# The first keys in two parts, and the sums, the spread and the first output block in other places: a change to a decode attention kernel

## The chip, the cores and the metric

The kernel runs on one core of a Trainium2 chip. The metric is the device time of one execution in microseconds (us). A profile is one execution taken by the hardware profiler; its span is some 2 us shorter than the time of the same run. "The change" is the edit under study, "the kernel before" is what it was made to.

## The reference, cut to what matters

One token attends over the last 4096 of 32768 cached positions in 32 heads; an MLP branch (not touched here) gates the result.

```python
W = min(4096, max(256, Sk // 4))
k = k_cache[:, :, Sk - W:, :]          # 32 heads x 4096 x 128, bf16: 33.6 MB
v = v_cache[:, :, Sk - W:, :]          # the same again
scores = einsum("bhqd,bhkd->bhqk", q, k) * Dh ** -0.5
p = softmax(scores)
o = einsum("bhqk,bhkd->bhqd", p, v)
s = o.reshape(B, Sq, Hq * Dh) @ wo     # wo is 4096 x 512
return x + s * g                       # g: the gate, from the MLP branch
```

## The kernel before

The 32 heads go in 8 groups of 4. A stage `s` does the scores of group `s`, the softmax of group `s-1` and the products with V of group `s-2`. Each group's keys (4.19 MB, 128 columns of rows) are split between two engines. VectorE does columns 0 to `nd` (64 or 80) in four quarters, each a product and a reduce (`k_vector`). TensorE transposes the rest in blocks of 8 columns (`k_turn`), ScalarE copies them out of PSUM, TensorE multiplies (`k_scores`).

```python
K_BUFS = 3; V_BUFS = 2                               # cut: other constants
ps_misc = tile_pool(name="ps_misc", bufs=1, space=PSUM)
ps_tr   = tile_pool(name="ps_tr",   bufs=3, space=PSUM)   # the transposes, tag "pt"

def sm_max(g):                                        # cut: VectorE, S <- own, m1 <- max of S
def sm_turn(g):
    mt_ps = ps_misc.tile([1, P], FP32, tag="misc", name="mt_ps")
    nc.tensor.transpose(mt_ps[:], s["m1"][:], ident_f[:])
    mx = sm_pool.tile([1, G], FP32, tag="mx", name="mx")
    nc.vector.tensor_reduce(out=mx[:], in_=mt_ps[:]...)   # cut; then md <- mx
def sm_exp(g):                                        # cut: mb_ps (misc) <- md on TensorE,
                                                      # 4 exponentials on ScalarE
def sm_den(g):
    s["den"] = ps_misc.tile([P, G], FP32, tag="misc", name="den_ps")
    nc.tensor.matmul(s["den"][:], lhsT=ones_f[:], rhs=s["sum"][:], start=True, stop=True)
def sm_rden(g):
    nc.vector.reciprocal(out=s["rden"][:], in_=s["den"][:])
```

`v_part` are the products with V. In groups 1 and 3 they are 32 wide matmuls into `ov`, whose result is put together one stage later. After group 3 the first 16 heads are done: `ox_spread(0)` (VectorE), `ox_pick(0)` (TensorE, then VectorE, over `ox_ps` in the misc pool) and `y_wide(0)` (16 wide matmuls into `yr_ps`) multiply them with the output weights in stage 6. In the code, `own` are the scores of TensorE's part, which ScalarE scales into SBUF; `mt_ps` is the transpose of the maxima, `mx` and `md` the maximum and its scaled negative for the exponentials; `spread` and `pick` bring the heads' outputs into the layout of the output weights. The order of this loop is the order of each engine's instructions:

```python
for s in range(NG + LAG):
    kn = load_kv(k_pool, A_k_cache, s) if s < NG else None
    # cut: loads of V, at the latest place the two V buffers allow
    if s < NG:
        k_vector(s, kn, 0); k_turn(s, kn, 0); k_turn(s, kn, 1); k_scores(s, 0)
        if s > 0:
            sm_turn(s - 1); k_turn(s, kn, 2); k_scores(s, 1); sm_exp(s - 1)
        # cut: v_add, v_out of groups 1 and 3
        if s == 6: ox_spread(0)
        k_vector(s, kn, 1)
        # cut: the remaining k_turn, k_scores
        sm_own(s)
        if s == 6: ox_pick(0)
        k_vector(s, kn, 2)
        if s > 0:
            sm_den(s - 1); sm_rden(s - 1)
        k_vector(s, kn, 3)
        if h >= 0: v_part(h, v)                       # h = s - 2
        sm_max(s)
        if s == 6: y_wide(0)
        # cut: v_out
    # cut: the two last stages
```

## Time and profile before

| | before |
|---|---|
| time, median of the 4 runs beside the change | 201.68 us (201.14 to 204.34) |
| span of the profile | 199.9 us |
| loads | 78.84 MB, 93.1% of the 16 DMA engines' time |
| VectorE busy | 73% |
| TensorE busy (matmul) | 67% |
| last V asked for | 178.05 us |

The highest of the four, 204.34, is 1.6% above the lowest and counts as slow; ratios leave such runs out, medians and ranges here do not.

The busy shares alone mislead: VectorE is the busiest compute engine, but the loads are busy nearly always. Which of them sets the end is read from the hole in the loads and from what the last loads wait for; the prediction shows these lines.

### The profile page before, as it was taken

How to read it: one execution, taken by the hardware profiler on the slowest of the kernel's cores; microseconds unless marked ns; L12 is line 12 of the kernel's file. 1: busy time of each engine (PE TensorE's matmuls, PEld its weight loads, DVE VectorE, ACT ScalarE, POOL GpSimd, SP SyncE). 2: the span in 40 equal slices, each digit the busy share in tenths (PEclk: the TensorE clock that was granted, in tenths of full speed). 3: DMA queues.
4: the chain of work that ended last, by engine and by line, in shares of the span. 5: the costliest groups of instructions: out<-in, count | busy, mean ns of one | idle time of the engine just before them, and what ended most of it. 6: DMA issues, size and time to landing. Idle time of an engine off the chain costs nothing.

```text
span 199.9 us, 4705 instructions
## 1 busy us (share of the span) xinstructions
PE 134.0 (67%) x2098; PEld 103.6 (52%) x2098; DVE 145.8 (73%) x160; ACT 85.3 (43%) x193; POOL 6.0 (3%) x13
## 2 busy tenths in 40 slices
PE   0459754953575268736997782789776876778582
PEld 0353544842465268635446782733576445766471
DVE  1640105999966999999999999999659999691201
ACT  2003004883687273528119752730792059723000
POOL 2110007000000000000000000000000000000000
PEclk9999855597555555555698755558965596555555
DMA  6999999999999999999999999999999999839850
GB/s 211 407 471 420 420 456 449 434 426 416 426 420 423 453 448 426 430 423 433 420 423 446 439 393 459 439 426 420 430 446 433 430 408 443 368 94 393 319 216 0
DMA packets 4891, 79.13 MB, mean 396 GB/s; under 512 B 648, under 2 KB 1512, under 8 KB 2024
## 3 DMA queue, kind: packets, MB, share of 16 engines
q1 hardware_dynamic: 4720, 78.84, 93.1%
q8 instruction: 16, 0.26, 0.5%
q10 hardware_dynamic: 152, 0.00, 0.0%
q14 instruction: 3, 0.02, 0.0%
HBM read 78.84 MB, written 0.00 MB: 394 GB/s over the span
## 4 chain that ended last, share of the span: by engine, by line
DVE 49%; PE 20%; DMA 16%; ACT 11%; issue 3%; ACTq 0%; DVEq 0%
DVE S L305 29%; DVE prod L303 15%; DMA kv<-in_A_k_cache_dram 14%; ACT kt L314 5%; PE ov L405 5%; ACT pT L357 4%; PE oT L413 4%; PE pt L312 4%; PE yr_ps L476 3%; PE sT L319 2%; DMA x_bf<-in_A_x_dram 2%; PE y_ps L152 1%; PE den_ps L363 1%; DVE S L333 1%; PE mb_ps L350 1%
## 5 line engine op out<-in xcount | busy, mean ns | idle before, releaser
L305 DVE TENSOR_REDUCE S<-prod 128x20 f32<-128x2560 bf16 (+1 forms) x32 | 83.8, 2619 | 1.1
L314 ACT COPY kt<-pt 128x1024 bf16<-128x1024 bf16 x54 | 53.3, 1013 | 18.5 <-PE pt L312 18.2
L312 PE MATMUL pt<-ident_bf,kv 128*128 128x128 bf16 x432 | 48.3, 286 | 3.5 <-DMA kv<-in_A_k_cache_dram 2.4
L303 DVE TENSOR_TENSOR prod<-kv,q_bc 128x2560 bf16<-128x2560 bf16 (+1 forms) x32 | 44.3, 1384 | 5.4 <-DMA kv<-in_A_k_cache_dram 5.1
L312 PEld LDWEIGHTS <-kv 128*128 128x128 bf16 x432 | 38.3, 130 | 5.7 <-issue 2.7
L319 PE MATMUL sT<-qT_bf,kt 128*128 128x4 bf16 x432 | 20.4, 169 | 18.6 <-ACT kt L314 18.3
L319 PEld LDWEIGHTS <-kt 128*128 128x128 bf16 x432 | 17.7, 107 | 24.6 <-ACT kt L314 24.1
L413 PEld LDWEIGHTS <-kv 128*128 128x128 bf16 x768 | 21.8, 104 | 2.2 <-issue 2.2
L413 PE MATMUL oT<-pT,kv 128*128 128x4 bf16 x768 | 21.5, 166 | 1.8 <-issue 1.8
L405 PE MATMUL ov<-kv,pT 128*16 128x512 bf16 x64 | 17.7, 447 | 0.0
L357 ACT ACTIVATE pT<-S,mb 128x128 bf16<-128x128 f32 x32 | 13.9, 568 | 0.2
L350 PE MATMUL mb_ps<-md,par_t 5*128 5x4 f32 x16 | 3.9, 311 | 13.2 <-DVE md L345 12.9
L405 PEld LDWEIGHTS <-pT 128*16 128x16 bf16 x64 | 6.4, 102 | 10.4 <-issue 5.1
L350 PEld LDWEIGHTS mb_ps<-md,par_t 5*128 5x128 f32 x16 | 3.4, 260 | 14.4 <-issue 12.5
L328 ACT ACTIVATE own<-sT,par 128x48 f32<-128x48 f32 (+1 forms) x32 | 7.6, 358 | 3.7 <-PE sT L319 3.7
L408 ACT COPY ov_sb<-ov 16x512 f32<-16x512 f32 x2 | 1.1, 574 | 16.6 <-PE ov L405 16.6
L357 ACT ACTIVATION_READ_ACCUMULATOR pT<-S,mb 128x1 f32 x32 | 8.1, 254 | 0.0
L432 DVE TENSOR_TENSOR o<-oT,rden 128x4 bf16<-128x4 f32 x2 | 0.3, 160 | 10.3 <-PE oT L413 10.3
L436 ACT ACTIVATE o<-oT,rden 128x1 bf16<-128x1 f32 x24 | 4.2, 255 | 8.4 <-PE oT L413 8.4
L368 DVE RECIPROCAL rden<-den_ps 128x4 f32<-128x4 f32 x8 | 1.4, 176 | 8.4 <-PE den_ps L363 8.4
L341 PE MATMUL mt_ps<-ident_f,m 128*1 128x128 f32 x8 | 2.7, 334 | 6.4 <-DVE m L335 6.4
L353 ACT COPY mb<-mb_ps 128x4 f32<-128x4 f32 x8 | 1.3, 164 | 13.1 <-PE mb_ps L350 13.1
(112 smaller groups left out, 89.5 us busy)
## 6 DMA issues: line engine op xcount, KB each, us to landing
kv<-in_A_k_cache_dram SPq DMA_DIRECT2D x8, 4096.0 KB, 23.1
kv<-in_A_v_cache_dram SPq DMA_DIRECT2D x7, 4096.0 KB, 27.5
wq_sb<-in_A_wq_dram SPq DMA_DIRECT2D x1, 4096.0 KB, 17.8
wo<-in_A_wo_dram SPq DMA_DIRECT2D x1, 2048.0 KB
kv<-in_A_v_cache_dram SPq DMA_DIRECT2D x1, 2048.0 KB, 9.1
w_sb<-in_B_w_dram SPq DMA_DIRECT2D x1, 1376.0 KB, 6.6
kv<-in_A_v_cache_dram SPq DMA_DIRECT2D x1, 1280.0 KB, 11.5
w_sb<-in_B_w_dram SPq DMA_DIRECT2D x1, 1024.0 KB, 8.8
```

The source lines that it names most:

```text
L303: nc.vector.tensor_tensor(out=prod[:, 0:m, :], in0=kn[:, rows, :], in1=q_bc[:, g:g + 1, :].to_broadcast([P, m, Dh]), op=ALU.mult)
L305: nc.vector.tensor_reduce(out=st[g]["S"][:, rows], in_=prod[:, 0:m, :], axis=AX.X, op=ALU.add)
L312: nc.tensor.transpose(pt[:, i, :], kn[:, nd(g) + 8 * b + i, :], ident_bf[:])
L314: nc.scalar.copy(out=kts[b][:], in_=pt[:])
L319: nc.tensor.matmul(st[g]["sT"][:, 8 * b + i, :], lhsT=kt[:, i, :], rhs=qT_bf[:, G * g:G * g + G], start=True, stop=True)
L328: nc.scalar.mul(s["own"][:, 0:m, a], s["sT"][:, 0:m, a], par[:, a:a + 1])
L350: nc.tensor.matmul(mb_ps[:], lhsT=par_t[:].rearrange("k b a -> k (b a)"), rhs=md[:], start=True, stop=True)
L357: nc.scalar.activation(out=s["pT"][:, :, a], in_=s["S"][:], func=ACT.Exp, scale=scale, bias=mb[:, a:a + 1], accum_out=s["sum"][:, a:a + 1])
L405: nc.tensor.matmul(s["ov"][:], lhsT=s["pT"][:, c:c + 4, :].rearrange("p i a -> p (i a)"), rhs=v[:, c:c + 4, :], start=(c == 0), stop=(c == ...
L413: nc.tensor.matmul(s["oT"][:], lhsT=v[:, c, :], rhs=s["pT"][:, c, :], start=(c == 0), stop=(c == CP - 1))
L436: nc.scalar.mul(o_blk[b][:, c + k:c + k + 1], st[g]["oT"][:, k:k + 1], st[g]["rden"][:, k:k + 1])
L476: nc.tensor.matmul(yr_ps[:], lhsT=ox_blk[i][:, t:t + 1], rhs=wo_blk[i][:, t, :], start=(t == 0), stop=(t == n - 1))
```

## The change

It is meant to take away four waits of VectorE: for the first keys (VectorE needs only their first half), for the sum over the partitions (`den`) in front of its reciprocal (the reciprocal moves to the next stage), for ScalarE's `o` in front of the spread (a quarter is put in front of it). The output block gets a PSUM buffer of the transposes' pool, because the misc buffer now stays taken. The first line of the diff only keeps the new load in two parts from starting row loads that belong to the last V. In the drain (`s == NG`) the last maxima's turn also goes in front of the spread.

```diff
-            if len(cuts) > 2 and c1 == cuts[-2]:
+            if len(cuts) > 3 and c1 == cuts[-2]:
...
-        yr_ps = ps_misc.tile([1, D], FP32, tag="misc", name="yr_ps")
+        yr_ps = ps_tr.tile([1, D], FP32, tag="pt", name="yr_ps")
...
-        kn = load_kv(k_pool, A_k_cache, s) if s < NG else None
+        kn = load_kv(k_pool, A_k_cache, s, (0, 64, CP) if s == 0 else (0, CP)) if s < NG else None
...
             k_scores(s, 0)
+            if s > 1:
+                sm_rden(s - 2)
             if s > 0:
                 sm_turn(s - 1)
...
-            if s == 6:
-                ox_spread(0)
             k_vector(s, kn, 1)
...
             if s == 6:
+                ox_spread(0)
+            k_vector(s, kn, 2)
+            if s == 6:
                 ox_pick(0)
-            k_vector(s, kn, 2)
             if s > 0:
                 sm_den(s - 1)
-                sm_rden(s - 1)
...
         elif s == NG:
+            sm_rden(NG - 2)
+            sm_turn(NG - 1)
             ox_spread(1)
-            sm_turn(NG - 1)
```

## The prediction

> **What bounds the kernel now.** I read the page's slices first, then the issues of the load queue (SP), then VectorE's timeline, then the chain of waits from 118 us on.
>
> ```profile
> DVE  1640105999966999999999999999659999691201
> DMA  6999999999999999999999999999999999839850
> ```
>
> One digit is 5 us. The transfers are busy from 5 to 170 us without a hole, at some 430 GB/s; the one hole is the 3, at 175 to 180 us. Compute that merely ends earlier in the middle shortens nothing by itself: 78.84 MB have to come in. To be won are the hole, the tail, and nothing else. By single microseconds (busy time of PE, PEld, DVE, ACT, POOL; granted clock, DMA share, GB/s):
>
> ```profile
> 173.00:174.00 1.00, 0.19 (x7) 0.20 (x8) 0.00 (x0) 0.75 (x1) 0.00 (x0) 0.50 0.92 385
> ...
> 176.00:177.00 1.00, 1.00 (x43) 1.00 (x41) 1.00 (x1) 0.00 (x0) 0.00 (x0) 0.50 0.25 87
> ...
> 179.00:180.00 1.00, 0.54 (x2) 0.07 (x2) 0.52 (x4) 0.00 (x0) 0.00 (x0) 0.50 0.73 131
> ```
>
> From 174 to 180 the six shares are 0.52, 0.50, 0.25, 0.04, 0.00 and 0.73, so 4.0 us of full transfer are lost; with the slow restart some 4.5. The cause is in the queue's own timeline:
>
> ```profile
> 156.10 0.58 SPq L79 DMA_DIRECT2D kv<-in_A_v_cache_dram  x1
> ...
> 178.05 1.88 SPq L79 DMA_DIRECT2D kv<-in_A_v_cache_dram  x3
> ```
>
> The values of the last group (7) are asked for only at 178.05, when all that was asked for before has drained. There are two V buffers, so they wait for TensorE's products with V of group 5 (174.47 to 178.05). From that issue to the last piece's products, 193.49 to 195.5, and to the end at 199.9, everything follows the load. **The end is the issue of the last V plus 22 us**, unless it comes before 174. So the question is how much earlier TensorE does group 5's products.
>
> VectorE's waits (last bracket: idle before, and what ended it):
>
> ```profile
> 32.37 1.23 DVE L303 TENSOR_TENSOR prod<-kv,q_bc 128x2048 bf16<-128x2048 bf16 x1 [5.05 <-DMA kv<-in_A_k_cache_dram]
> 61.59 0.18 DVE L368 RECIPROCAL rden<-den_ps 128x4 f32<-128x4 f32 x1 [3.42 <-PE den_ps L363]
> 147.00 0.43 DVE L443 TENSOR_TENSOR spread<-o,mt 128x256 bf16<-128x256 bf16 x1 [3.41 <-ACT o L436]
> 174.65 0.18 DVE L368 RECIPROCAL rden<-den_ps 128x4 f32<-128x4 f32 x1 [1.95 <-PE den_ps L363]
> ```
>
> These four are what the change is after; between them VectorE never rests, and stages 2 to 5 take 18.22 us each at its pace. But in stages 6 and 7 the chain of waits goes over TensorE and ScalarE:
>
> ```profile
> 131.86 9.09 PE ov L405 x32
> ...
> 147.00 0.43 DVE spread L443
> ...
> 151.68 0.34 DVE pick L453
> ...
> 157.02 5.04 PE yr_ps L476 x16
> ```
>
> **What the Trainium skill says.** "Perfetto Trace Analysis", Roofline, says that a single core's loads are bounded by its 16 DMA engines at about 435 GB/s. The trace agrees: stages 2 to 6 move 422 to 437 GB/s. "PSUM — Partial Sum Buffer", Engine vs sequencer instructions, says that [...]matmuls start in program order; so one blocked matmul holds all behind it. The trace agrees: TensorE idles 3.30 us before the maximum's broadcast at 125.28, with three blocks of transposes behind it whose keys had long landed (by the bytes, near 110). "TensorE: Matmul & The Clock Gate", Part 1, says that the clock doubles after some 3.4 us of sustained work, by a free-running window. The trace agrees in kind: the first-output products (L476) start at 157.02 with a granted clock of 0.50, and 1.00 is granted only from about 160; the same 32 products of L405 took 8.60 us in stage 3 and 9.15 in stage 5.
>
> **The change part by part.**
>
> *First keys in two parts.* VectorE needs only columns 0 to 63 of group 0. The whole 4.19 MB land at 32.3; half of that at 430 GB/s is 4.9 us, so the first part should land at about 27.5. The query copies end first at 29.57 + 0.59 = 30.2, and this now limits. VectorE starts 2.1 us sooner. TensorE's part still lands at 32.3.
>
> *The sum's reciprocal (rden).* In stage 1 it waited 3.42 us. Without it the last reduce of stage 1 ends at 59.6 (2.1 sooner plus 3.42), but then ScalarE's own-group scores are needed; they ended at 62.15, now 60.0. So 0.45 us come back as a new wait: VectorE is 3.42 + 2.15 - 0.5 = 5.1 us ahead after stage 1.
>
> *A new wait in each stage from 2 on.* The sum (den) stays in the misc PSUM pool, which has one buffer, until its reciprocal, now after the first quarter of the next stage. The transpose of the maxima (mt) takes the same buffer, and formerly ran beside that quarter; now it runs after the reciprocal while VectorE waits. The drain phase shows the price of that sequence:
>
> ```profile
> 178.62 0.29 DVE L335 TENSOR_REDUCE m<-S 128x1 f32<-128x128 f32 x1
> ...
> 179.37 0.28 DVE L343 TENSOR_REDUCE mx<-mt_ps 1x4 f32<-1x128 f32 x1 [0.33 <-PE mt_ps L341]
> ```
>
> 179.37 - 178.91 = 0.46 us from one small operation to the next over TensorE. With the reciprocal's 0.17 that is 0.64 per stage. Taking the reciprocal from its old place gives nothing back: from quarter 2 to 3 (with it) VectorE's starts are 4.38 us apart, from 1 to 2 (without) 4.37. Stages 2 to 4 thus cost 1.9, and VectorE enters stage 5 only 5.1 - 1.9 = 3.2 ahead. TensorE also has the third block of transposes behind the waiting mt; the exponentials come 1.35 us later relative to VectorE (mt 0.17, block 1.06, scores and sums about 0.2; before, the block was done long before). So the wide products of group 3 (9.15 us) start 3.2 - 1.35 = 1.8 ahead, at 130.0, and end at 139.1.
>
> *Spread and first output block.* In stage 6 VectorE's maxima wait for TensorE (turns after 139.1): they come at 141.3, also 1.8 ahead. Then quarter 1 (4.33), spread (0.43), quarter 2 (4.33): the pick reads at 150.5 to 150.9, formerly 151.60 to 152.01. So removing 3.41 us of wait makes the pick only 1.1 us earlier, because a quarter is now in front of it. The sum's matmul needs the pick's buffer, then the products of group 4 (3.55): they end at 155.0. The first output block has a buffer of its own now, and starts 0.96 us sooner behind them, at 154.9 for 157.02. Stage 7 on TensorE, where ScalarE is busy almost all through (162.1 to 175.2), starts 2.2 us ahead and keeps that: the last V at 175.9 for 178.05. The clock may rise a little earlier in the output block, as no idle time is in front of it; half of its cold time is 1.5 us, so I add 0.3.
>
> *Sum.* 2.1 (start) + 3.0 (stage 1) - 1.9 (new waits, stages 2 to 4) - 1.4 (TensorE later in stage 5) - 0.7 (pick behind a quarter) + 1.1 (output block) + 0.3 = 2.5 us. VectorE's 1.95 us of stage 7 are worth nothing at the end; the last group's maximum was ready near when TensorE was. From 202.0: 199.5.
>
> **Rivals.**
> 1. *The waits add up.* 2.1 + 3.4 + 3.4 + 1.95 = 10.9 us sooner, the last V asked for before 172: then the hole closes fully and the transfers cap the gain at 4.5 us: 197.5. For it: the hole is exactly behind this chain. Against it: the one misc buffer, and ScalarE and TensorE bounding stages 6 and 7.
> 2. *The keys arrive late.* By the bytes before them, groups 6 and 7 land at about 134 and 153.5; VectorE would be ready for them at about 135.5 and 156. In a slower stream that slack would be lost: a wait of up to 1 us, which stage 6's wait on TensorE mostly hides. 200.0.
> 3. *The new waits eat all.* If mt also collides with stages 4 and 6, where TensorE comes late from its wide products, and the clock falls back in the longer pauses, each of the two wide products can lose 0.5 us and the pick comes no sooner than now: 201.5 to 202. For it: the pick's gain of 1.1 us is the thinnest link.
>
> **Range and chances.** The middle path gives 2.5 us; rival 1 at most 4.5, rival 3 none, with the spread of the runs before (201.14 to 204.34) on top. I take 199.5, range 197.6 to 201.3. Over 2% faster needs 4 us, nearly the whole hole: 0.15. Slower needs new waits that exceed the gain: 0.03. The rest, 0.82.
>
> **What would show it.** Right: the first product at about 30.2; no wait in front of the reciprocals; a wait of about 0.45 us in front of mx in each of stages 2 to 5 and 2 us or so in stages 6 and 7; the pick near 150.5; the last V at 175 to 176; a smaller 3 in the DMA slices. Wrong: mx without a wait (the buffer doesn't bind) and the last V before 174, or a first product still at 32.

## The result, and the profile after

The change ran in 198.53 us (median of 4 runs, 198.31 to 199.75) beside 201.68. The ratio is 0.9863, with a 95% interval of 0.9817 to 0.9909: some 2.8 us better. A ratio is the mean time of one kernel's fast runs over that of the other's of the same rounds, so it is not quite the ratio of the medians. Later, 6 runs gave 0.9851 (0.9818 to 0.9883).

The slices of the changed kernel, 4.9 us each:

```profile
DVE  1540129979998899999989998999899967971201
DMA  6999899999999999999999999999999999968970
```

The hole in the loads is now a 6. Its issues of the last loads, from the queue's timeline:

```profile
155.28 0.58 SPq L79 DMA_DIRECT2D kv<-in_A_v_cache_dram  x1
...
175.90 1.88 SPq L79 DMA_DIRECT2D kv<-in_A_v_cache_dram  x3
```

The last V is asked for 2.15 us sooner (175.90 for 178.05). VectorE's waits in its timeline, the last bracket being the idle time before and what ended it:

```profile
28.60 1.23 DVE L303 TENSOR_TENSOR prod<-kv,q_bc 128x2048 bf16<-128x2048 bf16 x1 [2.17 <-ACT q_bc L253]
...
43.86 0.42 DVE L333 TENSOR_REDUCE S<-own 128x64 f32<-128x256 f32 x1 [0.97 <-ACT own L328]
...
59.47 0.42 DVE L333 TENSOR_REDUCE S<-own 128x64 f32<-128x256 f32 x1 [0.44 <-ACT own L328]
...
65.02 0.28 DVE L343 TENSOR_REDUCE mx<-mt_ps 1x4 f32<-1x128 f32 x1 [0.46 <-PE mt_ps L341]
...
103.53 0.28 DVE L343 TENSOR_REDUCE mx<-mt_ps 1x4 f32<-1x128 f32 x1 [1.25 <-PE mt_ps L341]
...
163.07 0.28 DVE L343 TENSOR_REDUCE mx<-mt_ps 1x4 f32<-1x128 f32 x1 [2.88 <-PE mt_ps L341]
```

All four old waits are gone from the stages; the first product now waits for the query copies (`q_bc`) instead of the keys. In their place VectorE waits for ScalarE's own-group scores (`own`) in stages 0 and 1 and for the transposed maxima (`mt_ps`) in every stage from 2 on. Why TensorE brings these late is told by its own timeline in stage 5:

```profile
121.98 0.37 PE L341 MATMUL mt_ps<-ident_f,m 128*1 128x128 f32 x1 [4.73 <-DVE rden L368]
122.15 1.06 PE L312 MATMUL pt<-ident_bf,kv 128*128 128x128 bf16 x8
```

TensorE stands 4.73 us for the reciprocal, with a block of transposes behind it. The chain of waits through stages 5 and 6 of the changed kernel (start, us, what):

```profile
130.21 9.19 PE ov L405 x32
...
146.28 0.33 DVE spread L443
...
150.87 0.34 DVE pick L453
...
155.25 5.17 PE yr_ps L476 x16
```

Against the lines of before: the wide products are 1.65 us sooner (131.86 to 130.21), the pick only 0.81, the output block 1.77.

From TensorE's last group 5 product to the end there were 21.9 us before and are 20.5 now. That part of the gain is in TensorE's timeline, before:

```profile
178.96 0.37 PE L341 MATMUL mt_ps<-ident_f,m 128*1 128x128 f32 x1 [0.94 <-DVE m L335]
...
186.95 0.93 PE L413 MATMUL oT<-pT,kv 128*128 128x4 bf16 x29 [0.90 <-issue]
...
190.90 1.65 PE L413 MATMUL oT<-pT,kv 128*128 128x4 bf16 x56
193.49 2.06 PE L413 MATMUL oT<-pT,kv 128*128 128x4 bf16 x72 [0.94 <-issue]
```

and after:

```profile
175.73 0.37 PE L341 MATMUL mt_ps<-ident_f,m 128*1 128x128 f32 x1
...
183.57 0.93 PE L413 MATMUL oT<-pT,kv 128*128 128x4 bf16 x29 [0.24 <-issue]
...
187.52 1.65 PE L413 MATMUL oT<-pT,kv 128*128 128x4 bf16 x56
190.10 2.06 PE L413 MATMUL oT<-pT,kv 128*128 128x4 bf16 x72 [0.93 <-issue]
```

Two things are to be seen. The transpose of the last maxima waited 0.94 us for VectorE and waits no longer. (Only 0.58 of it are won: TensorE's next work then waits 0.84 us for the spread, which needs ScalarE's `o` of group 5.) And the products stop twice in the middle of a group for "issue", that is for nothing that this view shows (t1 below tells what it is): after the 99th of 128 in group 6 (0.90 us before, 0.24 after) and after the 56th in group 7, in both kernels. The last V's first part has 64 columns, so a wait for data would stop after the 64th.

The chain of the changed kernel that ended last, from group 5's products on, has no load in it:

```profile
172.46 3.43 PE oT L413 x128
...
180.69 2.64 PE oT L413 x99
183.33 0.24 issue
183.57 0.95 PE oT L413 x29
...
187.59 1.58 PE oT L413 x56
189.17 0.93 issue
190.10 2.08 PE oT L413 x72
```

### The profile page after: what moved, and what is told of

Read it like the earlier page. It is cut to its first block, busy times and chain, and to the rows that moved or that the text cites. A ratio compares the mean times of both kernels' runs of the same rounds, so it can differ in the third digit from the quotient of the medians.

```text
span 196.4 us, 4710 instructions
## 1 busy us (share of the span) xinstructions
PE 133.2 (68%) x2098; PEld 102.6 (52%) x2098; DVE 146.6 (75%) x160; ACT 84.9 (43%) x193; POOL 6.0 (3%) x13
## 4 chain that ended last, share of the span: by engine, by line
PE 33%; DVE 29%; ACT 17%; DMA 16%; issue 3%; SPq 0%; ACTq 0%
DVE S L305 17%; DMA kv<-in_A_k_cache_dram 14%; PE ov L405 10%; ACT kt L314 9%; DVE prod L303 9%; PE oT L413 7%; PE pt L312 6%; ACT pT L357 4%; PE sT L319 3%; PE yr_ps L476 3%; DMA x_bf<-in_A_x_dram 2%; PE den_ps L363 1%; ACT own L328 1%; PE y_ps L152 1%; PE mt_ps L341 1%
## 5 line engine op out<-in xcount | busy, mean ns | idle before, releaser
L312 PE MATMUL pt<-ident_bf,kv 128*128 128x128 bf16 x432 | 46.7, 280 | 5.1 <-DMA kv<-in_A_k_cache_dram 4.2
L312 PEld LDWEIGHTS <-kv 128*128 128x128 bf16 x432 | 37.1, 127 | 7.3 <-DMA kv<-in_A_k_cache_dram 4.5
L319 PE MATMUL sT<-qT_bf,kt 128*128 128x4 bf16 x432 | 20.3, 169 | 20.1 <-ACT kt L314 19.8
L413 PEld LDWEIGHTS <-kv 128*128 128x128 bf16 x768 | 22.0, 105 | 1.5 <-issue 1.5
L405 PE MATMUL ov<-kv,pT 128*16 128x512 bf16 x64 | 19.0, 470 | 0.0
L343 DVE TENSOR_REDUCE mx<-mt_ps 1x4 f32<-1x128 f32 x8 | 2.2, 278 | 7.6 <-PE mt_ps L341 7.6
L341 PEld LDWEIGHTS mt_ps<-ident_f,m 128*1 128x1 f32 x8 | 0.6, 81 | 12.6 <-DVE rden L368 12.6
L226 DVE COPY hr<-hr_ps 1x512 f32<-1x512 f32 x1 | 0.7, 679 | 7.7 <-PE hr_ps L223 7.7
L363 PE MATMUL den_ps<-sum,ones_f 128*128 128x4 f32 x16 | 4.6, 357 | 2.5 <-DVE pick L453 1.9
```

The source lines that it names most:

```text
L312: nc.tensor.transpose(pt[:, i, :], kn[:, nd(g) + 8 * b + i, :], ident_bf[:])
L319: nc.tensor.matmul(st[g]["sT"][:, 8 * b + i, :], lhsT=kt[:, i, :], rhs=qT_bf[:, G * g:G * g + G], start=True, stop=True)
L405: nc.tensor.matmul(s["ov"][:], lhsT=s["pT"][:, c:c + 4, :].rearrange("p i a -> p (i a)"), rhs=v[:, c:c + 4, :], start=(c == 0), stop=(c == ...
L413: nc.tensor.matmul(s["oT"][:], lhsT=v[:, c, :], rhs=s["pT"][:, c, :], start=(c == 0), stop=(c == CP - 1))
```

## The experiments

What was open: how much each part of the change gives; whether the one misc buffer is behind the new waits; and whether the tail follows the last load, as the prediction had it, or a chain on TensorE. All twelve runs gave correct results. The ratios are to the kernel before in the same rounds. The times are medians of all runs, with those of before in brackets; times in the profile are from one run each.

| run | time | ratio (95%) | pick | last V asked for |
|---|---|---|---|---|
| the change | 198.53 (201.68) | 0.9863 (0.9817 to 0.9909) | 150.78 | 175.90 |
| u1_keys_whole | 201.65 (202.78) | 0.9969 (0.9904 to 1.0034) | 152.53 | 177.94 |
| u2_rden_back | 200.33 (202.78) | 0.9874 (0.9799 to 0.9949) | 151.27 | 176.70 |
| u3_spread_back | 200.15 (202.78) | 0.9886 (0.9841 to 0.9932) | 149.50 | 176.48 |
| a1_keys_only | 201.26 (202.78) | 0.9932 (0.9867 to 0.9997) | 151.81 | 178.18 |
| m1_max_buffer | 199.48 (202.50) | 0.9864 (0.9810 to 0.9918) | 149.44 | 175.30 |
| m2_max_pick_buffer | 198.16 (202.50) | 0.9781 (0.9727 to 0.9834) | 150.65 | 173.43 |
| m3_rows_early | 199.51 (202.50) | 0.9861 (0.9793 to 0.9928) | 151.76 | 177.11 |
| m4_all | 197.04 (202.50) | 0.9748 (0.9692 to 0.9805) | 149.14 | 171.90 |
| after_again | 199.33 (202.17) | 0.9851 (0.9818 to 0.9883) | 151.45 | 178.29 |
| a2_keys_block | 200.20 (202.17) | 0.9904 (0.9874 to 0.9934) | 150.97 | 176.99 |
| t1_more_instructions | 198.85 (202.17) | 0.9838 (0.9783 to 0.9893) | 149.91 | 177.42 |
| a3_buffers_only | 199.64 (202.17) | 0.9890 (0.9843 to 0.9937) | 149.48 | 176.08 |

A warning on single profiles: the same changed kernel asked for its last V at 175.90 in one profile and at 178.29 in another (after_again). Its first product began at 28.60 and 30.67, and its output block took 5.22 and 6.51 us. So a ranking within 1% rests on the ratios, and the profiles tell where waits are, not how large the gain is.

**u1_keys_whole**

```diff
-  kn = load_kv(k_pool, A_k_cache, s, (0, 64, CP) if s == 0 else (0, CP)) if s < NG else None
+  kn = load_kv(k_pool, A_k_cache, s) if s < NG else None
```

> The change with the first keys in one part again. My account (the end follows TensorE's group 5 products, which follow VectorE's place after stage 1): VectorE starts at about 32 instead of 28.6, stage 1's removed wait is worth 3.0, stages 2 to 4 lose 1.9, so the pick comes some 2.7 us later than in the changed kernel (about 153.4), the last V is asked for at about 178.5 and the time is about 201.2, hardly better than before. Rival, the loads bound the middle and the first keys are hidden anyway: the time stays at 198.5.

VectorE's first product is at 32.24, the pick at 152.53, the last V at 177.94. The ratio is 0.9969: without the first part's early landing hardly anything is left of the gain. That is as expected, and the rival (the first keys are hidden anyway) falls.

**u2_rden_back**

```diff
-  if s > 1: sm_rden(s - 2)
   ...
-  sm_den(s - 1)
+  sm_den(s - 1); sm_rden(s - 1)
   ...
-  sm_rden(NG - 2)
```

> The change with only the reciprocal of the sum back in its old place (the output block keeps its own buffer). My account: a wait of some 3.4 us comes back in stage 1, so VectorE is about 2.7 us ahead after it rather than 5.6, but the 0.65 us per stage in front of mx go away, and the exponentials are not 1.35 us late in stage 5: the pick comes at about 149.8 instead of 150.8, the last V is asked for at about 175, the time is about 197.5, that is 1 us better than the changed kernel. Rival, each removed wait counts: 3.4 + 1.95 us of VectorE come back and the time is 201 to 202.

The waits came back as expected (3.20 us in stage 1, none in front of mx in stages 2, 3 and 5). The ratio, 0.9874, is the changed kernel's within the noise. Its interval rules out 3 us worse; 1 us better (0.981) lies inside it, so the time does not refute my account, and nothing of that gain showed either. Two terms were missing from it. The wide products took 9.73 and 9.87 us in this profile, so mx waited for TensorE in stages 4 (0.73) and 6 (0.87). And in the tail the transpose of the maxima waited 0.94 us for VectorE again, with the drain's new order kept: the place of the reciprocal causes this wait, not the swap in the drain.

**u3_spread_back**

```diff
+  if s == 6: ox_spread(0)
   k_vector(s, kn, 1)
   ...
-  if s == 6: ox_spread(0)
-  k_vector(s, kn, 2)
   if s == 6: ox_pick(0)
+  k_vector(s, kn, 2)
```

> The change with only the spread and the pick of the first output block back in their old places. My account: VectorE waits some 3.4 us for ScalarE's o in stage 6 again, but the pick then comes after one quarter instead of two, at about 150.1 instead of 150.8; TensorE's group 4 products start 0.7 us sooner, the last V is asked for at about 175.2, and the time is 198.0, the same or 0.5 us better than the changed kernel. Rival, the removed 3.4 us counts: the time is about 201.5.

The wait in front of the spread was back (3.81 us), and the pick still came earlier, at 149.50: the quarter in front of the pick eats what the wait gave. The time is 0.9886, the same as the change within the intervals; the rival's 201.5 would be a ratio of 0.994, just outside the interval. The expected half microsecond of gain did not show: the output block took 6.12 us here. One line of VectorE's timeline, at the start of stage 6, matters for what follows:

```profile
135.83 1.49 DVE L303 TENSOR_TENSOR prod<-kv,q_bc 128x2560 bf16<-128x2560 bf16 x1 [0.80 <-DMA kv<-in_A_k_cache_dram]
```

VectorE was ready before the keys of group 6 had landed: a cap for anything that makes the stages before it faster.

**a1_keys_only**: the kernel before with the two parts of the first keys alone (the load's line of the diff and the guard in `load_kv`, nothing else).

> The kernel before with only the first keys in two parts. My account: VectorE starts about 2 to 3 us sooner, this goes through all stages unshortened (no new wait in front of mx), the last V is asked for at about 175.5 and the time is about 199.3: the first keys alone give most of what the whole change gives. Rival, the change's other two parts give the gain: 201.5.

The ratio is 0.9932 (some 1.4 us), between the two accounts: less than the 2.4 us expected. The shift did go through stages 1 to 3 (own-group reduces 1.7 us sooner). From stage 4 on it shrank to 0.6, because the wide products took 9.94 and 9.98 us in this profile for 8.60 and 9.15 before, and mx waited for them. So the first keys by themselves give about half of the change's gain, roughly, as the interval reaches from 0.9867 to 0.9997.

**m1_max_buffer**

```diff
-  mt_ps = ps_misc.tile([1, P], FP32, tag="misc", name="mt_ps")
+  mt_ps = ps_tr.tile([1, P], FP32, tag="pt", name="mt_ps")
```

> The change, with the transpose of the maxima in the pool of the key transposes, so that it no longer waits for the reciprocal. If the one misc buffer is what holds it, the 0.46 us in front of mx are gone in stages 2, 3 and 5, and VectorE stays some 5.5 us ahead up to stage 5. It then meets the keys of group 6, which landed at 135.8 in the run with the spread back: a wait for the load of 1 to 2.5 us at the start of stage 6. The pick comes at about 149.5 instead of 150.8; time about 197.2, some 1.3 us under the changed kernel. Rival, the wait in front of mx is the maxima's own path and not the buffer: no difference in it, 198.5.

The mechanism is shown: with another buffer for the transposed maxima there is no wait in front of mx in stages 2, 3 and 5. In VectorE's timeline of stage 3, and at the start of stage 6:

```profile
82.10 0.17 DVE L368 RECIPROCAL rden<-den_ps 128x4 f32<-128x4 f32 x1
82.19 0.25 DVE L343 TENSOR_REDUCE mx<-mt_ps 1x4 f32<-1x128 f32 x1
...
135.89 1.49 DVE L303 TENSOR_TENSOR prod<-kv,q_bc 128x2560 bf16<-128x2560 bf16 x1 [2.80 <-DMA kv<-in_A_k_cache_dram]
```

But the 2.8 us won were lost at once in the wait for group 6's keys, and the ratio, 0.9864, is the change's. The 1.3 us that I expected from the earlier pick did not show: the pick came 1.3 us earlier, but the output block took 6.00 us (5.22 in the change), and the stop in group 7 2.73 us (0.93).

**m2_max_pick_buffer**: m1 and

```diff
-  ox_ps = ps_misc.tile([P, n, n], FP32, tag="misc", name="ox_ps")
+  ox_ps = ps_tr.tile([P, n, n], FP32, tag="pt", name="ox_ps")
```

> The same, and the matmul of the first output block's pick in that pool too, so that the sum of group 5 and the products of group 4 don't wait for the pick. The products of group 4 come at about 146 to 149 instead of 151.7, the output block at about 150.6, stage 7 starts on TensorE at about 156 instead of 160.3, the last V is asked for at about 171.5, before the queue drains: the hole in the transfers closes. Then the load's end, at about 188, bounds the tail: time about 195.5 to 196.5. Rival, the tail is TensorE's chain alone: it moves by the full 4.5 us, to 194.

The products of group 4 began at 148.57 instead of 151.70 and the last V was asked for at 173.43. The ratio is 0.9781. Its slices of the loads:

```profile
DMA  6999999999999999999999999999999999999940
```

The hole is closed, as expected, but the time fell by 1.7 us against the change (0.9781 against 0.9863), less than the 2 to 3 expected, and the two intervals still overlap (up to 0.9834, from 0.9817). Group 6's products waited 1.03 us for their V, and the stop in group 7 was 2.46 us.

**m3_rows_early**

```diff
   load_rows(h_part, 2)
+  load_rows(H - 4, 2)
+  load_rows(H - 2, 2)
   v = load_kv(v_pool, A_v_cache, h, cuts)
-  load_rows(H - 2, 2)
```

(with the row load inside `load_kv` removed)

> The change, with the two last row loads of the output weights (0.52 MB, some 1.2 us of transfer) in front of the last V instead of between and behind its parts. They fill part of the hole. If the end follows the landing of the last load, as the prediction had it, the time falls by about 1 us, to 197.5. If it follows TensorE's chain after group 5's products, which the two traces suggest (both stall at the same matmul for instructions, not for data), nothing changes: 198.5, within 0.3.

The ratio is 0.9861 for 0.9863: no gain showed from 0.52 MB less to come in behind the last V's issue. The interval (0.9793 to 0.9928) also holds the 0.981 that the other account asks for, so the time alone does not decide. The profiles do. Take the stretch from the issue of the last V to the end of the span and subtract the stops for "issue" in it:

| kernels | last V to end, less the stops |
|---|---|
| reciprocal moved: the change, u1, u3, m1, m3, after_again, t1 | 19.2 to 19.4 us (m3 19.4, the change 19.3) |
| reciprocal in its old place: before, u2, a1, a2, a3 | 19.9 to 20.3 us |
| m2, m4 (products of group 6 wait 1.03 and 1.19 us for their V) | 20.1, 20.4 us |

With the load in front the tail of m3 is as long as without. So the tail of the changed kernel does not follow the last landing, which is against the prediction's sentence and for the chain on TensorE. Only in m2 and m4 does a load come into it.

**m4_all**: m2 and m3 together.

> The second with the third. If the hole is closed in the second already, the same bytes have to come in and the order hardly matters: within 0.5 us of the second kernel, 195.5 to 196.5.

The fastest kernel: 197.04 us, 0.9748. It beats the kernel before by 5.1 us and the change by 2.3 (0.9748 against 0.9863). It came 0.7 us under m2 where at most 0.5 was expected; the intervals of the two overlap widely.

**after_again**: the changed kernel unaltered, in the same rounds as the next three.

> The changed kernel again, beside the next one on the same chip, for a closer comparison: a ratio of 0.985 to 0.988.

0.9851, as expected.

**a2_keys_block**: the kernel before with the first keys in two parts and the output block's own buffer; the edits of u2 and u3 together. The drain keeps its new order.

> The kernel before with the first keys in two parts and the output block's own buffer, but neither the reciprocal nor the spread moved. The two runs that undid one of these moves alone were within 0.3% of the changed kernel, so if the moves are worth nothing, this is the changed kernel's time: a ratio of 0.985 to 0.989, with waits of about 3.4 us in front of the reciprocal of stage 1 and the spread. If the moves are worth something only together (each alone being masked by the other's wait), it lies between the run with the keys alone and the change: 0.991 to 0.993.

0.9904 (0.9874 to 0.9934), between the two accounts, against 0.9851 for the change in the same rounds: the moves of the reciprocal and the spread are worth some 1.1 us together, though each alone could be undone for 0.1 to 0.2%. The intervals overlap by a tenth of a per cent, so the size is rough; and whether one wait hid the other, or each alone was merely under the noise, is not shown. The buffer of the output block, in which a2 differs from a1 (besides the drain's order), is not told apart from noise either (0.9904 for 0.9932, in other rounds). TensorE's timeline shows one place where time is lost:

```profile
177.90 0.37 PE L341 MATMUL mt_ps<-ident_f,m 128*1 128x128 f32 x1 [0.94 <-DVE m L335]
```

The same wait of 0.94 to 1.03 us stood in every kernel with the reciprocal in its old place (before, u2, a1, a2, a3), and in none with it moved.

**t1_more_instructions**

```diff
-  rows_open(y_ps)
+  for _ in range(21):
+      rows_open(y_ps)
```

> The change with 20 more pairs of weight load and matmul in the preamble (the opening of the output sums with zeros, repeated; the result is unaffected). In all runs so far TensorE stalls in the tail after the 99th of group 6's 128 products and after the 56th or 57th of group 7's, 254 to 256 instructions apart, with nothing in the profile to wait for. If this is the refill of its instructions every 256, 40 more of them move both stalls 20 products earlier: after 79 and after 36 or 37. If they are waits for the last values or a power pause, they stay at 99 and 56. Time as the changed kernel's, within 1 us.

In TensorE's timeline of group 7:

```profile
188.64 1.12 PE L414 MATMUL oT<-pT,kv 128*128 128x4 bf16 x36
```

```profile
190.94 2.59 PE L414 MATMUL oT<-pT,kv 128*128 128x4 bf16 x92 [1.18 <-issue]
```

The stop moved from the 56th product to the 36th, exactly the 20 pairs put in front. It depends on the count of instructions, not on data. What it is can be read from the packed traces, which list every transfer: each of the 27 stops of this kind in the tails of the fourteen profiles ends 1.2 to 1.6 us after a 16 KB transfer of the instruction queue has ended (here one from 188.50 to 189.43, and the stop ends at 190.94). So TensorE waits for its instructions, and the stop is as long as their transfer is late. Of the other stop the expectation was half wrong: none showed at the 79th of group 6; one of 0.62 us showed after the 125th of group 5, which is again 256 instructions in front of that place. So the places follow the count, but not each of them shows a stop.

**a3_buffers_only**: m4 with the reciprocal and the spread in their old places.

> The fastest so far (all three small tiles in the transposes' pool, rows early) with the reciprocal and the spread back in their old places. VectorE loses 3.4 us in stage 1 again and is then some 2.7 us ahead of before, which lands it in stage 6 at 135.9, where the keys of group 6 come at about 135.8 anyway; and the pick comes after one quarter. If the load of the keys caps the middle, this is as fast as that kernel: 0.974 to 0.978. If the moved reciprocal counts by itself, it is 1 to 3 us slower: 0.98 to 0.99.

0.9890, the second case: the moves count by 2.9 us once the buffers are right. My reasoning took the landing of group 6's keys for the only limit. TensorE is another: its wide products of group 3 ended at 138.8 in this kernel and at 136.0 in m4. And in stage 7 the maxima's broadcast waited for VectorE, which had stood 3.41 us for the spread in stage 6:

```profile
163.61 0.37 PE L348 MATMUL mb_ps<-md,par_t 5*128 5x4 f32 x1 [2.86 <-DVE md L343]
```

## Why the prediction was right or wrong

The prediction was 199.5 us, 2.5 better than 202.0. Measured: 198.53, within the range, and a ratio that means 2.8 us. By its steps:

- *The last V waits for group 5's products, and these follow a chain over VectorE, TensorE and ScalarE.* Right. It had the last V at 175 to 176; the profile has 175.90.
- *First keys: 2.1 us.* The mechanism was right (the query copies limit, not the keys), the size off: 3.8 in this profile, 28.60 for 32.37. The 1.6 on top is in the preamble, where the query copies came at 27.98 instead of 29.57: an "issue" stop was shorter (0.73 for 1.43; it, too, ends 1.4 us after an instruction transfer in both), and the same 11 matmuls took 3.06 us for 3.77, for no reason that the profile shows. The edit touches nothing there, and in the profiles with split keys the first product lies between 28.60 and 30.71: this part is luck.
- *Stage 1: a new wait of 0.45 for the own-group scores.* Measured 0.44. A second one in stage 0 (0.97) was missing. VectorE was 65.12 - 59.47 = 5.65 us ahead after it; predicted 5.1.
- *The misc buffer costs 0.64 us a stage.* Right: waits of 0.46 and 0.46, and m1 shows the buffer to be the cause. In stage 4 it was 1.25, because the wide products took 9.73 us for 8.60. The lead into stage 5 was 120.42 - 117.50 = 2.9; predicted 3.2.
- *The exponentials come later behind a block of transposes.* Right: the wide products of group 3 began at 130.14, predicted 130.0.
- *The pick behind a quarter: 150.5.* Measured 150.78. In u3's profile, with the wait back, it came at 149.50: the removed wait gave the pick nothing.
- *Output block at 154.9, and 0.3 from the clock.* It began at 155.18; the clock gave nothing (5.22 us for 5.03).
- *VectorE's 1.95 us of stage 7 are worth nothing.* Wrong. With them gone the last maxima are ready when TensorE is, and the tail's first transpose no longer waits 0.94 us. The exponentials' broadcast follows the group 5 products after 1.63 us instead of 2.21, which is 0.6 us of the end.
- *The end is the issue of the last V plus 22 us, because all follows the load.* Wrong as to the cause. It was 21.9 before and 20.5 after, and 20.4 to 23.1 in all profiles. In the changed kernel the tail is a chain on TensorE: no load stands in it, and m3 brought the load forward for nothing. Its stops for instructions gave 0.66 us more in this pair of profiles (0.90 to 0.24). These stops vary from run to run, so that part is luck and not the change's.

The sum came out in part because errors cancel. VectorE started 1.7 us sooner than predicted, but stage 1 then gave 1.9 us for 3.0 (the wait of stage 0), and the waits of stages 2 to 4 cost 2.7 for 1.9. From there on the leads were close: 1.65 for 1.8 at group 3's products, 0.8 for 1.1 at the pick. The steps to the last V gave 2.15 for 2.5, and the tail gave 0.6 that was taken for nothing. Rival 1 (the waits add up to 4.5) fell: the change got 2.8. Rival 2 (the keys arrive late) was no cost in the change, where VectorE came to stage 6 at 136.37, but it is the next limit, seen in u3, m1, m2 and m4. Rival 3 fell as well.

What stays open: the exact worth of the reciprocal's and of the spread's move (each alone is under the noise of these rounds; of the reciprocal's, the tails above show 0.5 to 1.1 us), and why the transfer of instructions comes early in one run, for a stop of 0.24 us, and late in another, for one of 2.73.

## What to carry to other kernels

Moving a wait's consumer to a later place keeps its buffer taken for longer; look at once for who takes that buffer next, and give the small tile a buffer of a pool that turns over anyway. A wait removed on an engine counts only as far as the next thing on the chain (here another engine's products, then the landing of the keys), so follow the chain to the event that starts the last load, and then check by moving the load itself whether the tail follows it; where the time is too noisy to tell, compare the tails in the profiles. Two moves can each look worthless when undone alone, within the noise; undo them together before calling them so.

## What the Trainium skill lacked or had wrong

- "Runtime: NRT & Kernel Launch", Instruction fetch mechanics, says that instructions are refilled in 16 KiB blocks of 256 and that crossing a boundary is mostly hidden. The runs agree with the 256 (stops 254 to 256 instructions apart, and one moved by 20 pairs when 20 pairs were put in front). They differ on the cost: in the tail a stop took 0.24 to 2.73 us, and it lay on the path that sets the end. That it is the refill is seen in the transfers: each stop ends 1.2 to 1.6 us after a 16 KB transfer of the instruction queue.
- "TensorE: Matmul & The Clock Gate", Part 1, says that the ramp is under 1% of a typical span and run-variable. The runs agree that it varies: the same 32 wide matmuls took 8.53 to 9.98 us and the same 16 of the output block 5.01 to 6.51. The share can be larger: one execution has two of the former and one of the latter, so their spread adds up to 4.4 us, 2% of the span, if all come out slow; in a1 one slow set took 1.1 us off VectorE's lead.
- No page that I read gives a time for what a PSUM buffer costs that is held by a late reader: the one of the misc pool cost VectorE 0.46 us of waiting in stages 2 and 3 and 0.47 in stage 5, and taking the transposes' pool instead (m1) took this away.
